# Q of batches 2 to 7 loaded four tokens to a partition, and read with a stride by the score matmuls

## The chip, the cores and the metric

One Trainium2 chip; the kernel runs on one of its cores. The metric is the time of one execution on the device, in microseconds. Before the change it was 320.49 us (median of 3 runs, 319.1 to 322.19). Runs of one kernel scatter by about 0.5%, so differences under 2% are read here only from several rounds on one chip.

## The reference

Sliding-window causal attention, then a two-layer MLP with a hard-swish gate. Cut to what matters:

```python
B, H, S, D = 8, 8, 576, 64            # q, k, v: [B, H, S, D] float32, about 0.1 in size
scores = (q @ k.T) / sqrt(D)          # only 0 <= query - key < 64 is kept
attn = softmax(scores) @ v            # per batch and head
x = attn.transpose(0, 2, 1, 3).reshape(B * S, H * D)     # 4608 tokens of 512
h = x @ w_in                          # w_in [512, 2048]
g = h * clip(h + 3, 0, 6) / 6
out = g @ w_out                       # w_out [2048, 512]
```

## The kernel before

Everything on TensorE is bf16. A batch has 576 tokens: 512 "main" ones (`SM`) and a tail of 64 (`SR`). The 4608 tokens pass through the MLP in nine blocks of 512. While block T is computed, the attention of batch T+1 is interleaved with it on TensorE, from T = 1 to 6; the last two blocks have no attention beside them.

Batches 0 and 1 are transposed by TensorE. Batches 2 to 7, the ones that the change touches, come in by DMA, are cast on GpSimd (`pcopy`) and transposed by DMA from `qn`, `kn` into `QT`, `KT`. These hold one row per head dimension (two heads on 128 partitions) and one column per token.

```python
P, R, SM, SR = 128, 4, 512, 64
QW = 192                               # queries that one block of 128 keys can see

def load_blocks(t, src, b, kbs, tail=0):
    ...                                # block kb: token kb*128 + p goes to partition p
        out.append(nc.sync.dma_start(
            out=t[p0 : p0 + ss, kb, :, :],
            in_=src[b, :, s0 : s0 + ss, :].rearrange("h s d -> s h d"),   # runs of 64 f32 = 256 B
        ))

def load_for_dma(b):                   # batches 2 to 7
    for n, src in (("qst", q), ("kst", k), ("vst", v)):
        t = stage.tile([P, KB, H, D], F32, name=n, tag=n)
        ins += load_blocks(t, src, b, range(KB), ...)

def transpose_by_dma(self):
    for n, T in ((qn_all, self.QT), (kn_all, self.KT)):
        nc.sync.dma_start_transpose(out=T[:]..., in_=n[:]...)

def scores(bt, g, u, ...):             # g: pair of heads; u: which half of the key blocks
    ...                                # (o0, k0, q0, n): column in PSUM, first key, first query, queries
    blocks = (
        ((0, 0, 0, QW), (QW, P, P, QW)),
        ((0, 2 * P, 2 * P, QW), (QW, 3 * P, 3 * P, P), (QW + P, S - P, SM, SR)),
    )[u]
    for o0, k0, q0, n in blocks:
        for h in range(2):             # heads on partitions 0-63 and 64-127: they run side by side
            nc.tensor.matmul(
                st[:, h, o0 : o0 + n],
                lhsT=bt.KT[h * D : (h + 1) * D, g, k0 : k0 + P],
                rhs=bt.QT[h * D : (h + 1) * D, g, q0 : q0 + n],     # contiguous columns
                ...)
    def exps():                        # ScalarE, PSUM -> SBUF
        nc.scalar.activation(out=pT[:, :, 2 * u : 2 * u + 2, 0:QW],
            in_=st[:, :, 0:w].rearrange("p h (k w) -> p h k w", k=2), func=EXP, scale=scale)
```

So a pair of heads needs ten score matmuls: five pairs with 192, 192, 192, 128 and 64 columns, 768 in all for each head. That the two of a pair run side by side shows in the trace: all ten take 0.44 us (below), and one after another, at the 0.42 ns per column of the MLP's matmuls (216 ns from start to start for 512), the 1536 columns would take 0.65.

The softmax here doesn't subtract the row's maximum and nothing guards it: scores larger than these inputs give would overflow.

Of the kernel before, what the change touches and what calls it, by code (L numbers as in the profile page):

```python
# [9 lines left out]
F32 = mybir.dt.float32  # L10
# [14 lines left out]
def kernel(  # L25
# [9 lines left out]
    nc = tc.nc  # L35
    P = nc.NUM_PARTITIONS
    B, H, S, D = q.shape
# [4 lines left out]
    KB = (S + P - 1) // P  # L42
    SP = KB * P
    R = 4
    SM = P * R
    SR = S - SM
# [4 lines left out]
    QW = P + WINDOW  # L51
# [4 lines left out]
    stage = ctx.enter_context(tc.tile_pool(name="stage", bufs=1))  # L56
# [31 lines left out]
    def load_blocks(t, src, b, kbs, tail=0):  # L88
        out = []
        for kb in kbs:  # L90
            s0 = kb * P
            ss = min(P, S - s0)
            p0 = tail if ss < P else 0
            out.append(nc.sync.dma_start(  # L94
                out=t[p0 : p0 + ss, kb, :, :],
                in_=src[b, :, s0 : s0 + ss, :].rearrange("h s d -> s h d"),
            ))
        return out

    def load_qk_for_pe(b, heads):  # L100
        qst = stage.tile([P, H, R * D], F32, name="qst", tag="qst")
        kst = stage.tile([P, H, R * D], F32, name="kst", tag="kst")
        rst = stage.tile([P, H, D], F32, name="rst", tag="rst")
        ins = []
        for h0 in range(0, H, heads):
            for dst, src in ((qst, q), (kst, k)):
                ins.append(nc.sync.dma_start(
                    out=dst[:, h0 : h0 + heads, :],
                    in_=src[b, h0 : h0 + heads, 0:SM, :].rearrange("h (p j) d -> p h (j d)", j=R),
                ))  # L110
            if h0 == 0:
                for i, src in enumerate((q, k)):
                    ins.append(nc.sync.dma_start(
                        out=rst[i * SR : (i + 1) * SR, :, :],
                        in_=src[b, :, SM:S, :].rearrange("h s d -> s h d"),
                    ))
        return (qst, kst, rst), ins
# [5 lines left out]

    def load_for_dma(b):
        sts, ins = [], []
        for n, src in (("qst", q), ("kst", k), ("vst", v)):
            t = stage.tile([P, KB, H, D], F32, name=n, tag=n)
            ins += load_blocks(t, src, b, range(KB), SR if src is v else 0)
            sts.append(t)
        return tuple(sts), ins  # L130

    ctx.enter_context(tc.manual_schedule())
    def load_first():
# [28 lines left out]
    def keep_busy(n):  # L162
# [11 lines left out]
        out=mask1[:], in_=mask1[:], pattern=[[1, QW]], compare_op=ISGE,  # L174
# [3 lines left out]
        out=mask1[:], in_=mask1[:], pattern=[[-1, QW]], compare_op=ISGE,  # L178
        fill=0.0, base=WINDOW - 1, channel_multiplier=1,
    )  # L180
    qn_all = consts.tile([P, NG, KB, 2, D], BF16, name="qn")
    kn_all = consts.tile([P, NG, KB, 2, D], BF16, name="kn")
# [3 lines left out]
    for o0, m0, m1 in ((0, 0, QW), (QW, 0, QW), (2 * QW, 0, QW), (3 * QW, 0, P), (3 * QW + P, WINDOW, P)):  # L186
        nc.vector.tensor_scalar(
            out=maskneg[:, o0 : o0 + m1 - m0], in0=mask1[:, m0:m1],
# [45 lines left out]
    vcopy, pcopy, acopy = nc.vector.tensor_copy, nc.gpsimd.tensor_copy, nc.scalar.copy  # L234

    class Batch:
# [10 lines left out]
            copy(out=self.V[SR:P, KB - 1, :, 0:D], in_=vst[SR:P, KB - 1, :, :])  # L247

        def cast_for_dma(self, st, which=(0, 1, 2)):
            for n, s in [((qn_all, st[0]), (kn_all, st[1]))[i] for i in which if i < 2]:  # L250
                for g in range(NG):
                    pcopy(  # L252
                        out=n[:, g, 0 : KB - 1, :, :].rearrange("p k h d -> p k (h d)"),
                        in_=s[:, 0 : KB - 1, 2 * g : 2 * g + 2, :].rearrange("p k h d -> p k (h d)"),
                    )
                pcopy(
                    out=n[:SR, :, KB - 1, :, :].rearrange("p g h d -> p g (h d)"),
                    in_=s[:SR, KB - 1, :, :].rearrange("p (g h) d -> p g (h d)", h=2),
                )
            if 2 in which:  # L260
                self.cast_v(st[2], 0, H, pcopy)
                self.cast_v_end(st[2], pcopy)
# [66 lines left out]
    def scores(bt, g, u, bias=False, bank=None):  # L329


        pT = P_ring[(bt.b * NG + g) % NPT]
        st = ps_st.tile([P, 2, 512], F32, name=f"st{u if bank is None else bank}")
        w = 2 * QW
        if bias:
            for h in range(2):
                nc.tensor.matmul(
                    st[:, h, 0:w], lhsT=ident[:], rhs=maskneg[:, u * w : (u + 1) * w],
                    start=True, stop=False,
                )  # L340
        blocks = (
            ((0, 0, 0, QW), (QW, P, P, QW)),
            ((0, 2 * P, 2 * P, QW), (QW, 3 * P, 3 * P, P), (QW + P, S - P, SM, SR)),
        )[u]
        for o0, k0, q0, n in blocks:
            for h in range(2):
                nc.tensor.matmul(  # L347
                    st[:, h, o0 : o0 + n],
                    lhsT=bt.KT[h * D : (h + 1) * D, g, k0 : k0 + P],
                    rhs=bt.QT[h * D : (h + 1) * D, g, q0 : q0 + n],  # L350
                    start=not bias, stop=not bias or o0 == blocks[-1][0],
                )

        def exps():
            nc.scalar.activation(  # L355
                out=pT[:, :, 2 * u : 2 * u + 2, 0:QW],
                in_=st[:, :, 0:w].rearrange("p h (k w) -> p h k w", k=2),
                func=EXP, scale=scale,
            )

        return exps
# [180 lines left out]
    def S_(bt, g, u):  # L542
        later[bt.b, "s", g, u] = scores(bt, g, u)
# [33 lines left out]
    bt, st = Batch(0), stage0  # L577
# [12 lines left out]
    def S0_(g, u):  # L590
        later[0, "s", g, u] = scores(bt, g, u, bias=True, bank=(u if g > 1 else g))
# [50 lines left out]
    st1, ins = load_qk_for_pe(1, 4)  # L642
    for x in ins:
# [5 lines left out]
        out=mask[:], in_=mask1[:].unsqueeze(1).to_broadcast([P, 2 * (KB - 1), QW])  # L649
    )  # L650
    for h in range(2):
        nc.vector.tensor_copy(
            out=mask[:, (KB - 1) * (h + 1) - 1, P:QW], in_=mask1[:, WINDOW : 2 * WINDOW],
        )
    bt, st = Batch(1), st1
# [14 lines left out]
    for g in range(NG):  # L670
        bt.cast_v(vst1, 2 * g, 2 * g + 2, pcopy)
    st2, _ = load_for_dma(2)

    m = s2(0, BY_QUARTER)
# [80 lines left out]
    for T in range(1, NTB):  # L755
        p1, p2 = pieces(nxt)
        b = T + 2
        nxt = None
        if b < B:
            sts, _ = load_for_dma(b)  # L760
            nxt = Batch(b)
            p1.setdefault(12 if T == 1 else 6, []).append(
                lambda bt=nxt, sts=sts: bt.cast_for_dma(sts)
            )
            p2.setdefault(6 if T == 1 else 12, []).append(lambda bt=nxt: bt.transpose_by_dma())
        stage_(T, None, p1, p2)
# [30 lines left out]
```

## Time and profile before

| | before |
|---|---|
| time, median | 320.49 us |
| span of the profiled run | 317.6 us |
| TensorE busy | 300.8 us (95%) |
| DMA packets under 512 B | 138272 |
| one full period (a block of the MLP and one batch of attention) | 32.0 us |
| ten score matmuls of a head pair | 0.44 us |

The first lines are from the profile's page: busy time of the engines, and the DMA packets.

```profile
PE 300.8 (95%) x2131; PEld 149.5 (47%) x2167; DVE 173.9 (55%) x331; ACT 177.9 (56%) x265; POOL 85.7 (27%) x131
...
DMA packets 150843, 52.64 MB, mean 166 GB/s; under 512 B 138272, under 2 KB 146464, under 8 KB 150816
```

The next are from the table of stretches of the same kernel: each line is a stretch (start and end in us), its length, then busy us and instructions of TensorE, its weight loads, VectorE, ScalarE and GpSimd, the granted clock of TensorE, the DMA share and GB/s. The first three stretches are full periods, the last is a block without attention.

```profile
162.53:194.57 32.04, 31.83 (x234) 15.85 (x237) 19.72 (x36) 19.17 (x29) 9.71 (x13) 1.00 1.04 203
194.57:226.60 32.03, 31.82 (x234) 15.87 (x237) 19.93 (x36) 19.17 (x29) 10.27 (x13) 1.00 1.02 201
226.60:258.64 32.04, 31.83 (x235) 15.86 (x237) 19.31 (x36) 19.17 (x29) 0.00 (x0) 1.00 0.37 79
258.64:286.27 27.63, 27.52 (x127) 12.54 (x128) 11.00 (x16) 13.34 (x20) 0.00 (x0) 1.00 0.10 39
```

TensorE has no gaps there. The first two stretches and the third take the same 32.0 us although the DMA share falls from 1.04 to 0.37: in this part DMA doesn't set the pace.

Where DMA does reach TensorE is the timeline of TensorE, in three places. Each line has start, length, what ran, and in brackets the idle time just before it and what ended that.

```profile
76.59 0.51 PE L347 MATMUL st<-QT,KT 64*128 64x192 bf16 x10 [0.43 <-DMA KT<-kn]
...
106.69 0.51 PE L347 MATMUL st<-QT,KT 64*128 64x192 bf16 x10 [1.97 <-DMA KT<-kn]
...
130.77 1.46 PE L466 MATMUL st<-xT,win 128*128 128x512 bf16 x6 [1.04 <-DMA xT<-opg]
```

These 3.4 us are what earlier loads could win. From 131 us on TensorE waits for no DMA. The price of a score group stands in the same timeline, inside a period:

```profile
171.96 0.51 PE L347 MATMUL st<-QT,KT 64*128 64x192 bf16 x10
172.40 1.04 PE L466 MATMUL hT<-xT,win 128*128 128x512 bf16 x3
```

A length (0.51) reaches past the next start (171.96 + 0.51 = 172.47), so lengths overlap; the cost is the distance of the two starts, 172.40 - 171.96 = 0.44 us for 768 columns.

### The profile page before, as it was taken

Reading aid. Unit: us, or ns where it says so; the run is one execution under the profiler, and the core shown is the slowest. Engines: PE = TensorE matmul, PEld = TensorE weight load, DVE = VectorE, ACT = ScalarE, POOL = GpSimd, SP = SyncE. Lnnn points to the kernel's source line nnn. Section 1 sums busy time; section 2 is a strip of 40 time slices with the busy share of each in tenths; the row PEclk is TensorE's granted clock in tenths of the full one; section 3 lists DMA queues with packets and bytes.
Section 4 is the critical chain, followed back from the end, with each engine's and each line's share of the span. In section 5 each row is a group of like instructions: output and inputs, shape, how many; then the busy total and the mean of one; then the engine's idle time right before and its main releaser. Section 6 shows DMA issues by size and latency. Waiting matters only on the chain.

```text
span 317.6 us, 5604 instructions
## 1 busy us (share of the span) xinstructions
PE 300.8 (95%) x2131; PEld 149.5 (47%) x2167; DVE 173.9 (55%) x331; ACT 177.9 (56%) x265; POOL 85.7 (27%) x131
## 2 busy tenths in 40 slices
PE   8989799999999799899999999999999999999995
PEld 3454345544554355344544554445444544444442
DVE  4658643476636665277527853785378438406700
ACT  2748753387637771487258725872587347417711
POOL 5741805363045143305610650065000000000000
PEclk9999999999999999999999999999999999999999
DMA  8999999999799999999999998999800630010011
GB/s 211 237 173 253 238 199 205 204 184 248 158 208 209 270 215 205 191 254 204 195 257 210 207 184 208 211 201 185 204 34 2 122 75 0 28 73 33 0 68 66
DMA packets 150843, 52.64 MB, mean 166 GB/s; under 512 B 138272, under 2 KB 146464, under 8 KB 150816
## 3 DMA queue, kind: packets, MB, share of 16 engines
q1 hardware_dynamic: 146000, 46.77, 72.7%
q0 software_dynamic: 4544, 5.24, 9.5%
q8 instruction: 17, 0.28, 0.4%
q10 hardware_dynamic: 272, 0.26, 0.2%
q14 instruction: 10, 0.08, 0.1%
HBM read 36.70 MB, written 9.44 MB: 145 GB/s over the span
## 4 chain that ended last, share of the span: by engine, by line
PE 63%; DMA 21%; SPq 8%; POOL 3%; issue 2%; DVE 1%; ACT 1%; POOLq 0%
PE o L503 15%; PE acc L503 14%; PE hT L466 14%; PE acc L466 5%; PE o L466 5%; SPq L94 5%; DMA vst<-in_v_dram 4%; DMA kst<-in_k_dram 4%; DMA KT<-kn 4%; DMA qst<-in_q_dram 3%; PE st L466 3%; PE st L347 3%; DMA wout<-in_moe_w_out_dram 3%; DMA win<-in_moe_w_in_dram 3%; PE hT L377 1%
## 5 line engine op out<-in xcount | busy, mean ns | idle before, releaser
L466 PEld LDWEIGHTS <-win 128*128 128x128 bf16 x576 | 55.3, 98 | 67.2 <-issue 2.3
L503 PEld LDWEIGHTS <-gT 128*128 128x128 bf16 x576 | 52.9, 98 | 57.5 <-issue 0.6
L503 PE MATMUL o<-wout,gT 128*128 128x512 bf16 x274 | 67.5, 379 | 1.5 <-DMA wout<-in_moe_w_out_dram 0.7
L503 PE MATMUL acc<-wout,gT 128*128 128x512 bf16 x278 | 67.1, 379 | 0.7 <-issue 0.3
L466 PE MATMUL hT<-xT,win 128*128 128x512 bf16 x266 | 65.7, 379 | 0.3
L355 ACT ACTIVATE pT<-st 128x768 bf16<-128x768 f32 x64 | 48.9, 813 | 10.8 <-PE st L347 10.7
L473 ACT ACTIVATE t<-hT,half 128x512 bf16<-128x512 f32 x68 | 46.7, 690 | 9.6 <-PE hT L466 9.2
L474 DVE SCALAR_TENSOR_TENSOR gT<-t,hT 128x512 bf16<-128x512 bf16 x68 | 46.4, 685 | 9.4 <-ACT t L473 9.1
L474 DVE SCALAR_TENSOR_TENSOR gT<-t,st 128x512 bf16<-128x512 bf16 (+1 forms) x26 | 19.7, 768 | 52.9 <-ACT t L473 52.9
L365 DVE TENSOR_TENSOR pT<-pT,mask 128x1536 bf16<-128x1536 bf16 x28 | 28.1, 1004 | 23.0 <-ACT pT L355 23.0
L509 ACT COPY osb<-o 128x512 f32<-128x512 f32 x18 | 10.6, 586 | 46.2 <-PE o L503 46.2
L252 POOL CAST qn<-qst 128x512 bf16<-128x512 f32 x24 | 16.1, 712 | 74.1 <-DMA qst<-in_q_dram 59.7
L509 ACT COPY osb<-acc 128x512 f32<-128x512 f32 x18 | 10.6, 587 | 35.7 <-PE acc L503 33.7
L466 PE MATMUL st<-xT,win 128*128 128x512 bf16 x117 | 28.2, 379 | 1.7 <-DMA xT<-opg 1.0
L397 DVE TENSOR_TENSOR opg<-hT,rec 128x320 bf16<-128x320 f32 x56 | 27.5, 492 | 1.9
L466 PE MATMUL acc<-xT,win 128*128 128x512 bf16 x91 | 23.6, 379 | 0.1
L466 PE MATMUL o<-xT,win 128*128 128x512 bf16 x90 | 23.5, 379 | 0.1
L473 ACT ACTIVATE t<-st,half 128x512 bf16<-128x512 f32 (+1 forms) x26 | 19.4, 752 | 7.2 <-PE st L466 7.1
L377 PEld LDWEIGHTS <-pT 128*128 128x128 bf16 x256 | 17.8, 97 | 9.1 <-issue 1.4
L347 PE MATMUL st<-QT,KT 64*128 64x192 bf16 (+2 forms) x320 | 17.9, 229 | 4.2 <-DMA KT<-kn 2.4
L394 DVE RECIPROCAL rec<-hT 128x5 f32<-128x5 f32 x56 | 10.5, 188 | 20.0 <-PE hT L386 19.9
L243 POOL CAST V<-vst 128x512 bf16<-128x512 f32 (+1 forms) x14 | 16.4, 1168 | 17.4 <-DMA vst<-in_v_dram 17.0
(76 smaller groups left out, 269.2 us busy)
## 6 DMA issues: line engine op xcount, KB each, us to landing
out_dram<-osb SPq DMA_DIRECT2D x32, 256.0 KB, 2.4
qst<-in_q_dram SPq DMA_DIRECT2D x28, 256.0 KB, 4.7
kst<-in_k_dram SPq DMA_DIRECT2D x27, 256.0 KB, 5.4
vst<-in_v_dram SPq DMA_DIRECT2D x24, 256.0 KB, 5.1
vst<-in_v_dram SPq DMA_DIRECT2D x24, 128.0 KB, 4.1
win<-in_moe_w_in_dram POOLq DMA_DIRECT2D x4, 512.0 KB, 7.6
wout<-in_moe_w_out_dram POOLq DMA_DIRECT2D x4, 512.0 KB, 8.8
qst<-in_q_dram SPq DMA_DIRECT2D x2, 512.0 KB, 6.1
```

Source lines behind the costliest of these rows:

```text
L243: copy(out=self.V[:, 0 : KB - 1, h0:h1, 0:D], in_=vst[:, 0 : KB - 1, h0:h1, :])
L252: pcopy(out=n[:, g, 0 : KB - 1, :, :].rearrange("p k h d -> p k (h d)"), in_=s[:, 0 : KB - 1, 2 * g : 2 * g + 2, :].rearrange("p k h d -> ...
L347: nc.tensor.matmul(st[:, h, o0 : o0 + n], lhsT=bt.KT[h * D : (h + 1) * D, g, k0 : k0 + P], rhs=bt.QT[h * D : (h + 1) * D, g, q0 : q0 + n], ...
L355: nc.scalar.activation(out=pT[:, :, 2 * u : 2 * u + 2, 0:QW], in_=st[:, :, 0:w].rearrange("p h (k w) -> p h k w", k=2), func=EXP, scale=scale,
L365: nc.vector.tensor_tensor(out=pT[:, :, :, 0:QW], in0=pT[:, :, :, 0:QW], in1=mask[:].rearrange("p (h k) w -> p h k w", h=2), op=MULT,)
L377: nc.tensor.matmul(ob, lhsT=pT[:, h, qb, 0:P], rhs=V[:, qb, 2 * g + h, :], start=True, stop=(qb == 0),)
L397: nc.vector.tensor_tensor(out=opgs[bt.b, g][:, :, h, :], in0=ov[:, :, 0:D], in1=rec[:].unsqueeze(2).to_broadcast([P, KB, D]), op=MULT,)
L466: nc.tensor.matmul(hT, lhsT=win16[:, g, fc * P : (fc + 1) * P], rhs=xT[:, g, t0 : t0 + TB], start=(g == 0), stop=(g == NG - 1),)
L473: nc.scalar.activation(out=t1[:], in_=hT, func=RELU, bias=half[:], scale=1.0 / 6.0)
L474: nc.vector.scalar_tensor_tensor(out=out, in0=t1[:], scalar=1.0, in1=hT, op0=MIN, op1=MULT,)
L503: nc.tensor.matmul(accs[ts], lhsT=gT[:, fc, ts * P : (ts + 1) * P], rhs=wout16[:, fc, :], start=(fc == 0), stop=(fc == NFC - 1),)
L509: nc.scalar.copy(out=osb[:], in_=accs[ts])
```

## The change

The intent is fewer, longer packets. If partition p takes the four consecutive tokens 4p to 4p+3, each head gives one run of 1 KB in place of four of 256 B, and three loads of Q are issued in place of five. The price is the order: after the DMA transpose token 4s+j stands in column 128j+s. The scores undo this by reading Q^T with a step of 128 columns (256 bytes) for j within s. The 64 tail tokens stay in natural order. K and V stay as they were.

```diff
     def load_for_dma(b):
-        for n, src in (("qst", q), ("kst", k), ("vst", v)):
+        qst = stage.tile([P, H, R * D], F32, name="qst", tag="qst")
+        rst = stage.tile([P, H, D], F32, name="rst", tag="rst")
+        for h0 in range(0, H, 4):
+            ins.append(nc.sync.dma_start(
+                out=qst[:, h0 : h0 + 4, :],
+                in_=q[b, h0 : h0 + 4, 0:SM, :].rearrange("h (p j) d -> p h (j d)", j=R),
+            ))
+        ...  # the tail into rst
+        for n, src in (("kst", k), ("vst", v)):
...
             # cast_for_dma
+                        pcopy(
+                            out=n[:, g, 0 : KB - 1, :, :],
+                            in_=st[0][0][:, 2 * g : 2 * g + 2, :].rearrange("p h (j d) -> p j h d", j=R),
+                        )
...
             # scores
+        if bt.b > 1:
+            for i in range(2):
+                for h in range(2):
+                    kb = 2 * u + i
+                    n = min(QW, SM - kb * P)
+                    nc.tensor.matmul(
+                        st[:, h, i * QW : i * QW + n].rearrange("p (s j) -> p s j", j=R),
+                        lhsT=bt.KT[h * D : (h + 1) * D, g, kb * P : (kb + 1) * P],
+                        rhs=bt.QT[h * D : (h + 1) * D, g, 0:SM].rearrange(
+                            "d (j s) -> d s j", j=R
+                        )[:, kb * P // R : (kb * P + n) // R, :],
+                        start=True, stop=True,
+                    )
+            ...  # the 64-column tail, contiguous, as before
-        for o0, k0, q0, n in blocks:
+        for o0, k0, q0, n in blocks if bt.b < 2 else ():
```

The matmuls and weight loads are the same ones in the same order; only the access pattern of one operand differs.

More of the change, by code (lines that the diff above doesn't have):

```diff
@@ L125, in load_for_dma @@
         sts, ins = [], []
-        for n, src in (("qst", q), ("kst", k), ("vst", v)):
+        qst = stage.tile([P, H, R * D], F32, name="qst", tag="qst")
[5 more added lines that the diff above has]
+            ))
+        ins.append(nc.sync.dma_start(
+            out=rst[0:SR, :, :], in_=q[b, :, SM:S, :].rearrange("h s d -> s h d"),
+        ))
+        for n, src in (("kst", k), ("vst", v)):
             t = stage.tile([P, KB, H, D], F32, name=n, tag=n)
@@ L129, in load_for_dma @@
             sts.append(t)
-        return tuple(sts), ins
+        return ((qst, rst), *sts), ins
     ctx.enter_context(tc.manual_schedule())
@@ L249, in cast_for_dma @@
         def cast_for_dma(self, st, which=(0, 1, 2)):
-            for n, s in [((qn_all, st[0]), (kn_all, st[1]))[i] for i in which if i < 2]:
+            for i in which:
+                if i > 1:
+                    continue
+                n = (qn_all, kn_all)[i]
                 for g in range(NG):
-                    pcopy(
-                        out=n[:, g, 0 : KB - 1, :, :].rearrange("p k h d -> p k (h d)"),
-                        in_=s[:, 0 : KB - 1, 2 * g : 2 * g + 2, :].rearrange("p k h d -> p k (h d)"),
-                    )
+                    if i:
+                        pcopy(
+                            out=n[:, g, 0 : KB - 1, :, :].rearrange("p k h d -> p k (h d)"),
+                            in_=st[1][:, 0 : KB - 1, 2 * g : 2 * g + 2, :].rearrange("p k h d -> p k (h d)"),
+                        )
+                    else:
+                        pcopy(
+                            out=n[:, g, 0 : KB - 1, :, :],
+                            in_=st[0][0][:, 2 * g : 2 * g + 2, :].rearrange("p h (j d) -> p j h d", j=R),
+                        )
+                rest = st[1][:SR, KB - 1, :, :] if i else st[0][1][:SR, :, :]
                 pcopy(
                     out=n[:SR, :, KB - 1, :, :].rearrange("p g h d -> p g (h d)"),
-                    in_=s[:SR, KB - 1, :, :].rearrange("p (g h) d -> p g (h d)", h=2),
+                    in_=rest.rearrange("p (g h) d -> p g (h d)", h=2),
                 )
@@ L340, in scores @@
                 )
+        if bt.b > 1:
[10 more added lines that the diff above has]
+                        start=True, stop=True,
+                    )
+            if u:
+                for h in range(2):
+                    nc.tensor.matmul(
+                        st[:, h, QW + P : 2 * QW],
+                        lhsT=bt.KT[h * D : (h + 1) * D, g, S - P : S],
+                        rhs=bt.QT[h * D : (h + 1) * D, g, SM:S],
+                        start=True, stop=True,
+                    )
         blocks = (
```

## The prediction

> **What bounds the kernel now.** TensorE: 300.8 of 317.6 us busy (95%, busy table). In the table of stretches each full period from 162 us on (one token block of the MoE plus one batch of attention) lasts 32.0 us with PE busy 31.8, at full clock. PE's 17 us of idle time lie before 131 us. DMA looks full there (share about 1 until 230 us), but only three of PE's waits are ones that Q loading can touch (timeline of PE): 0.43 us before the first scores of batch 2 (76.6 us, released by the K transpose), 1.97 us before those of batch 3 (106.7 us, same releaser), 1.04 us at 130.8 us (released by the transpose into xT). Together 3.4 us.
>
> **What it removes.** For each of six batches, the 1 MB main part of Q goes from 4096 packets of 256 B to 1024 of 1 KB. In the trace's packets of the hardware queue these take 22.5 and 57 ns on average, so 5.8 us of the sixteen engines become 3.6 (an estimate). SyncE issues three Q loads in place of five (5 to 6 us a batch in its timeline; I expect 2.5 to 4). K, V and the transposes behind them should come 2 to 3 us sooner, enough to erase the three waits: about -3 us. After 131 us an earlier load is worth nothing.
>
> **What it moves.** Nothing in order: the same matmuls and weight loads; GpSimd's reordered Q cast has the form that takes 0.62 us in batch 0.
>
> **What it adds.** The moving operand of the scores of batches 2 to 7 is read in steps of 256 bytes, apart from the 64-column tail. The ten score matmuls of a head pair take 0.44 us (timeline): five pairs side by side, 768 columns, 704 of them now strided; 24 groups x 704 = 16,900 columns, 7.0 us at 2.4 columns per ns. Four of the six batches lie wholly in the PE-bound part and pay in full. The Trainium skill, "SBUF — State Buffer", note on cachelines, says that each access to a new 16-byte line pays a penalty and that two hits per line are needed to absorb the latency; it gives no figure for TensorE. No instruction of this trace reads a strided moving operand, so this is the gamble:
> - no penalty: about 317.5 us (chance 0.3)
> - half rate: +0.29 us per group, +7.0 - 3.2, about 324 (0.4)
> - quarter rate or worse: +21 - 3, about 338 (0.25)
> - between: 0.05
>
> **Prediction.** 323.5 us, 8 in 10 between 316.5 and 336. Faster by over 2%: 0.03; within 2%: 0.70; slower by over 2%: 0.27.
>
> **What would show each step.** Packets under 512 B fall by about 24,600, under 2 KB by 18,400. The waits at 76, 106 and 130 us shrink below 0.3 us each. Score groups of batches 2 to 7: 0.44 us if the stride is free, about 0.73 at half rate, 1.3 at quarter rate; the period 32.0, 33.2 or 35.5 us. The last two blocks, without attention, stay at 27.6 us each.
>
> **What would make it wrong.** The stride costing more than half rate, or breaking the side-by-side running of two heads; the two-level step pattern costing extra; 1 KB pieces draining no faster because HBM binds; a much slower cast on GpSimd.

## The result, and the profile after

338.19 us (median of 4 runs, 336.26 to 339.52) against 321.34 us before (median of 4, 319.1 to 322.19); ratio 1.0531, 95% interval 1.0448 to 1.0615. A ratio here is the mean time of one kernel's fast runs over the mean of the other's of the same rounds, so it is not quite the ratio of the medians. The change is slower by 5%, outside the predicted range (316.5 to 336).

The page of the kernel after, the same two lines:

```profile
PE 321.9 (96%) x2131; PEld 152.1 (45%) x2167; DVE 174.9 (52%) x331; ACT 182.1 (54%) x265; POOL 87.1 (26%) x131
...
DMA packets 132219, 52.64 MB, mean 157 GB/s; under 512 B 113504, under 2 KB 127840, under 8 KB 132192
```

The packets fell as meant, by 24,768 under 512 B. TensorE is busy 21.1 us longer with the same 2131 recorded matmuls. The table of stretches of the kernel after, three full periods and the block without attention:

```profile
169.34:204.90 35.56, 35.35 (x235) 16.28 (x237) 20.09 (x36) 20.02 (x29) 10.34 (x13) 1.00 0.79 181
204.90:240.45 35.55, 35.34 (x234) 16.26 (x237) 19.62 (x36) 20.02 (x29) 10.33 (x13) 1.00 0.85 181
240.45:276.00 35.55, 35.34 (x235) 16.25 (x237) 19.57 (x36) 20.02 (x29) 0.00 (x0) 1.00 0.31 72
276.00:303.63 27.63, 27.52 (x128) 12.54 (x128) 11.00 (x16) 13.33 (x20) 0.00 (x0) 1.00 0.10 39
```

A period with attention takes 3.5 us more; the block without attention takes exactly what it took. The timeline of TensorE after, one score group (the tail now has a line of its own):

```profile
178.77 1.35 PE L366 MATMUL st<-QT,KT 64*128 64x192 bf16 x8
179.95 0.21 PE L376 MATMUL st<-QT,KT 64*128 64x64 bf16 x2
180.09 1.04 PE L507 MATMUL hT<-xT,win 128*128 128x512 bf16 x3
```

The group takes 180.09 - 178.77 = 1.32 us in place of 0.44. Its 704 strided columns take 1.18 us, 1.68 ns each; 24 groups x 0.88 us = 21.1 us. The spans differ by 335.3 - 317.6 = 17.7 us, 3.4 us less, which is what the three waits were; all three are gone (the same three places, now without a bracket):

```profile
76.46 1.35 PE L366 MATMUL st<-QT,KT 64*128 64x192 bf16 x8
...
107.67 1.35 PE L366 MATMUL st<-QT,KT 64*128 64x192 bf16 x8
...
133.63 1.89 PE L507 MATMUL st<-xT,win 128*128 128x512 bf16 x8
```

That the sum closes to a tenth is partly luck: other waits moved as well (for V from GpSimd 2.1 us in place of 1.3), and in this execution the granted clock was 0.93 and 0.90 from 30 to 40 and from 40 to 50 us, where it had been 1.00. It looks as if the loads had paid their part. The experiments show that this reading is only half right.

### The profile page after: what moved, and what is told of

The parts are those of the page before. It is cut to its first block, busy times and chain, and to the rows that moved or that the text cites. A ratio compares the mean times of both kernels' runs of the same rounds, so it can differ in the third digit from the quotient of the medians.

```text
span 335.3 us, 5584 instructions
## 1 busy us (share of the span) xinstructions
PE 321.9 (96%) x2131; PEld 152.1 (45%) x2167; DVE 174.9 (52%) x331; ACT 182.1 (54%) x265; POOL 87.1 (26%) x131
## 4 chain that ended last, share of the span: by engine, by line
PE 85%; DMA 7%; ACT 2%; SPq 2%; issue 1%; DVE 1%; POOL 1%; POOLq 0%
PE o L544 19%; PE acc L544 18%; PE hT L507 16%; PE st L366 9%; PE acc L507 6%; PE o L507 6%; PE st L507 5%; DMA win<-in_moe_w_in_dram 2%; DMA kst<-in_k_dram 2%; PE hT L418 2%; PE hT L423 1%; DMA vst<-in_v_dram 1%; DMA qst<-in_q_dram 1%; PE hT L448 1%; DVE gT L515 1%
## 5 line engine op out<-in xcount | busy, mean ns | idle before, releaser
L544 PE MATMUL o<-wout,gT 128*128 128x512 bf16 x274 | 68.3, 382 | 1.0 <-issue 0.2
L271 POOL CAST qn<-qst 128x512 bf16<-128x512 f32 x24 | 14.8, 645 | 72.8 <-DMA qst<-in_q_dram 72.8
L366 PE MATMUL st<-QT,KT 64*128 64x192 bf16 x192 | 32.5, 469 | 0.0
L266 POOL CAST kn<-kst 128x512 bf16<-128x512 f32 x24 | 16.6, 729 | 28.1 <-DMA kst<-in_k_dram 24.0
```

The source lines that it names most:

```text
L266: pcopy(out=n[:, g, 0 : KB - 1, :, :].rearrange("p k h d -> p k (h d)"), in_=st[1][:, 0 : KB - 1, 2 * g : 2 * g + 2, :].rearrange("p k h d ...
L271: pcopy(out=n[:, g, 0 : KB - 1, :, :], in_=st[0][0][:, 2 * g : 2 * g + 2, :].rearrange("p h (j d) -> p j h d", j=R),)
L366: nc.tensor.matmul(st[:, h, i * QW : i * QW + n].rearrange("p (s j) -> p s j", j=R), lhsT=bt.KT[h * D : (h + 1) * D, g, kb * P : (kb + 1) ...
L544: nc.tensor.matmul(accs[ts], lhsT=gT[:, fc, ts * P : (ts + 1) * P], rhs=wout16[:, fc, :], start=(fc == 0), stop=(fc == NFC - 1),)
```

## The experiments

In all of them "strided" means the read of Q^T in steps of 128 columns. The comparison with the reference passed for every run, also for those that take the tokens in a wrong order: q and k are so small that the softmax weights are nearly equal and the order hardly shows in the output. So a pass says little about the order here. The kernel before and three of these were therefore also evaluated in a simulation of their values (not of their times), with q and k 15 times larger: the relative error was 0.0055 for the kernel before and for both kernels below that are meant to be right (`e_act`, `e_psumw`), and 1.09 for `e_contig`, which is meant to be wrong. When this document was checked, the simulation was repeated: it gave the same figures, and 0.0055 for the change itself.

The theory: the stepped read costs TensorE time by itself. Rivals: the new loads or casts cost it; any two-level pattern costs it; the two heads no longer run side by side.

### The loads alone: `e_contig`

```diff
-    st[:, h, i * QW : i * QW + n].rearrange("p (s j) -> p s j", j=R),
+    st[:, h, i * QW : i * QW + n],
     lhsT=bt.KT[h * D : (h + 1) * D, g, kb * P : (kb + 1) * P],
-    rhs=bt.QT[..., g, 0:SM].rearrange("d (j s) -> d s j", j=R)[:, kb * P // R : (kb * P + n) // R, :],
+    rhs=bt.QT[h * D : (h + 1) * D, g, kb * P : kb * P + n],      # wrong order on purpose
```

> The change's loads (1 KB runs of Q), but the scores of batches 2 to 7 read Q^T without a stride, so the tokens stand in the wrong order and the result is wrong on purpose. Theory (the strided read costs, the loads help a little): score groups back at 0.44 us, period 32.0 us, the waits at 76, 106 and 130 us gone or under 0.5 us, time about 318 us, ratio to before 0.985 to 0.995. Rival (the new loads, casts or their contention cost the time): about 338 us, ratio 1.05, with score groups at 0.44 us and waits elsewhere. Rival 2 (the waits vanished only because the slower scores delay TensorE): ratio 0.997 to 1.003, the waits still there.

Measured: 317.55 us (6 runs) against 320.44 us; ratio 0.9905, interval 0.9861 to 0.9948. TensorE waits for no K transpose and no transpose into xT in the whole run. The scores of batch 3 start here with no wait before them:

```profile
104.21 1.03 PE L505 MATMUL hT<-xT,win 128*128 128x512 bf16 x4
105.17 0.48 PE L366 MATMUL st<-QT,KT 64*128 64x192 bf16 x8
105.48 0.19 PE L374 MATMUL st<-QT,KT 64*128 64x64 bf16 x2
```

The K transpose of batch 2 was issued at 69.06 us and landed 6.6 us later, before 76.16 us, when TensorE had been ready for it in the kernel before (76.59 less the wait of 0.43).

What follows: the new loads cost nothing and win about 1% when the scores are not slowed. The rivals "the loads cost" and "the waits vanish only because TensorE is late" both fall for this kernel.

### The stride alone: `e_stride_only`

```diff
 # the kernel before, with its own loads and casts
+        if bt.b > 1:
+            ...  # the strided score matmuls of the change; wrong order on purpose
-        for o0, k0, q0, n in blocks:
+        for o0, k0, q0, n in blocks if bt.b < 2 else ():
```

> The loads of before, with the strided read of the scores in batches 2 to 7 (wrong token order, wrong result on purpose). Theory: score groups 1.3 us, period 35.5 us, time about 338 to 341 us, ratio 1.053 to 1.065, at or a little above the whole change, because the waits at 76 and 130 us may stay. Rival (the loads cost): about 321 us, ratio 1.00.

Measured: 338.83 us (4 runs) against 320.44 us; ratio 1.0561, interval 1.0505 to 1.0617. This is the whole loss. More: it is the time of the whole change (1.0531, interval 1.0448 to 1.0615), with the loads of before, and here too no wait for a K transpose or for xT is left on TensorE. The scores of batch 3 start at 109.47 us in place of 106.69, right behind the matmuls ahead of them; slower scores of batch 2 have made TensorE late enough for the old loads (the first line is the first scores of batch 2):

```profile
78.26 1.36 PE L346 MATMUL st<-QT,KT 64*128 64x192 bf16 x8
...
108.51 1.03 PE L487 MATMUL hT<-xT,win 128*128 128x512 bf16 x4
109.47 0.81 PE L346 MATMUL st<-QT,KT 64*128 64x192 bf16 x4
```

What follows: the two effects are not a sum. The stride alone removes the two longer waits, 1.97 and 1.04 us. The third, 0.43 us before the first scores of batch 2, comes ahead of every strided read, so its absence here is not the stride's doing: in this execution TensorE was 2.2 us late already at the last scores of batch 1 (49.30 us against 47.07; the granted clock was 0.83 from 40 to 50 us, against 1.00). The better loads remove all three, but once the stride has removed two, the 0.4 us that is left is less than these runs could show. The two ratios come from different jobs, so a difference of some tenths of a per cent stays open.

### Which patterns cost: `e_sweep`

Each of the 24 score groups reads Q^T with another pattern, in one run; matmul counts and sizes are unchanged.

```diff
+    STEPS = {  # by batch and head pair
+        (2, 0): ("step", 1), (2, 1): ("step", 2), (2, 2): ("step", 3), (2, 3): ("far", 128, 4),
+        (3, 0): ("step", 1), (3, 1): ("step", 4), (3, 2): ("step", 6), (3, 3): ("step", 8),
+        (4, 0): ("step", 5), (4, 1): ("step", 7), (4, 2): ("step", 12), (4, 3): ("step", 13),
+        (5, 0): ("runs", 4, 8), (5, 1): ("runs", 2, 8), (5, 2): ("runs", 2, 12), (5, 3): ("runs", 4, 32),
+        (6, 0): ("far", 4, 48), (6, 1): ("far", 8, 24), (6, 2): ("far", 32, 6), (6, 3): ("far", 64, 4),
+        (7, 0): ("h0",), (7, 1): ("h1",), (7, 2): ("long",), (7, 3): ("keys",),
+    }
-                        rhs=bt.QT[...].rearrange("d (j s) -> d s j", j=R)[...],
+                        rhs=rhs,       # built from STEPS; wrong order on purpose
```

"step n" is one column in n; "runs m, n" is m contiguous columns in every n; "far n, m" has steps of n columns inside and of one column outside; "long" is four runs of 48 (or 32) columns, 128 apart; "h0" and "h1" stride one head only (by 128); "keys" reads the stationary K in steps of 13 columns and Q without.

> The change's loads, and in each of the 24 score groups of batches 2 to 7 another access pattern of the moving operand (wrong result on purpose). A group's eight 192- and 128-column matmuls (704 columns in pairs) take about 0.33 us from the first start to the start of the tail at full rate, 0.6 at half and 1.18 at quarter rate. Theory A (every access that opens a new 16-byte line costs four column times): steps of 2, 3 and 4 elements 0.33 us, or up to 0.6 for 4; steps of 8, 12 and 13 all 1.18; two-level patterns with 2 or 4 elements per line 0.33 to 0.6; four runs of 48 with 128 between them 0.33; four elements 8 or more apart 1.18. Theory B (the two-level step pattern costs, whatever the distance): single steps of 8 to 13 0.33, all two-level ones 1.18. Theory C (the two heads no longer run side by side and each goes at half rate): groups in which only one head is strided about 0.16 x 3.7 + 0.08 x 3.7 = 0.9 us; under A they take 1.18, the slower head's time. A strided stationary operand (last group) with contiguous moving: 0.33 to 0.5.

Measured, as the distance from the first start of the eight wide matmuls (704 columns) to the start of the tail:

| pattern | bf16 columns per 16-byte line | us | ns per column |
|---|---|---|---|
| step 1; long | 8 | 0.31 to 0.32 | 0.45 |
| runs 4, 8 and 4, 32 | 4 | 0.32 | 0.45 |
| step 3 | 2.7 | 0.48 | 0.68 |
| step 4; runs 2, 8 and 2, 12; far 4 | 2 | 0.61 to 0.62 | 0.87 |
| step 5 | 1.6 | 0.76 | 1.08 |
| step 6 | 1.3 | 0.92 | 1.31 |
| step 7 | 1.1 | 1.08 | 1.53 |
| step 8, 12, 13; far 8 | 1 | 1.22 to 1.26 | 1.73 to 1.79 |
| far 32, 64, 128 | 1 | 1.17 to 1.18 | 1.66 to 1.68 |
| keys (stationary strided) | 8 (moving) | 0.35 | 0.50 |

Step 2 (4 columns per line) had a wait on ScalarE in the middle, so it gives only a part: its last 320 columns took 0.14 us, 0.44 ns each. Theory A had put a step of 3 at 0.33 us; it took 0.48. Whole lines for step 4 and step 8 of this run:

```profile
112.02 0.79 PE L410 MATMUL st<-QT,KT 64*128 64x192 bf16 x8
112.63 0.21 PE L420 MATMUL st<-QT,KT 64*128 64x64 bf16 x2
...
118.86 1.41 PE L410 MATMUL st<-QT,KT 64*128 64x192 bf16 x8
120.09 0.21 PE L420 MATMUL st<-QT,KT 64*128 64x64 bf16 x2
```

What follows: the cost is that of a line, not of a stride. A line of 16 bytes costs about 1.7 ns, the time of four columns at full rate (216 ns start to start for 512 columns is 0.42 ns each), and its columns are free up to four. Steps that give one column per line cost about four times the full rate's time (1.66 to 1.79 ns against 0.45), whether the step is 16 bytes or 256. That a pattern has two levels costs nothing ("runs 4, 8", "long"). With one head strided the wide matmuls and the tails of the group took 246.11 - 244.79 = 1.32 us, as with both, and so did the group with the other head strided. If the heads excluded each other, then of the wide matmuls' time with both strided each head would have half, at half the rate, and a head read at the full rate would need only half of its half: three quarters in all. In that group one head's tail even starts before the other head's last wide matmuls:

```profile
244.79 0.81 PE L410 MATMUL st<-QT,KT 64*128 64x192 bf16 x6
245.11 0.20 PE L420 MATMUL st<-QT,KT 64*128 64x64 bf16 x1
245.43 0.72 PE L410 MATMUL st<-QT,KT 64*128 64x192 bf16 x2
245.97 0.20 PE L420 MATMUL st<-QT,KT 64*128 64x64 bf16 x1
246.11 1.04 PE L551 MATMUL hT<-xT,win 128*128 128x512 bf16 x3
```

The Trainium skill, "SBUF — State Buffer", note on cachelines, asks for two hits per line. For TensorE's moving operand in bf16 two hits gave half the rate and 2.7 two thirds of it; four gave the full rate. The strided stationary operand ("keys") is not free either. Its eight weight loads took 136 ns in the median against 94 in the group "long" (from the view of the tile KT; shortest/median/longest in ns, first and last start in us, "keys" first); of that, 0.04 us reached the group, which took 0.35 us against 0.31:

```profile
L410 PEld LDWEIGHTS <-KT x8: 136/136/157, 256.4 to 256.7; 64*128 64x128 bf16 x8
...
L410 PEld LDWEIGHTS <-KT x8: 92/94/95, 252.8 to 253.0; 64*128 64x128 bf16 x8
```

The time of this run (330.51 us, one look) is that of a mixture and isn't used.

### The stride moved to the write into PSUM: `e_psumw`

```diff
-    st[:, h, i * QW : i * QW + n].rearrange("p (s j) -> p s j", j=R),
+    st[:, h, i * QW : i * QW + n].rearrange("p (s j) -> p j s", j=R),
-    rhs=bt.QT[...].rearrange("d (j s) -> d s j", j=R)[:, kb * P // R : (kb * P + n) // R, :],
+    rhs=bt.QT[...].rearrange("d (j s) -> d j s", j=R)[:, :, kb * P // R : (kb * P + n) // R],
```

> The change's loads with a correct result: TensorE reads Q^T as four runs of 48 (or 32) tokens and writes the scores to PSUM with a step of four columns (16 bytes), so PSUM holds the natural order and the exponential stays as it was. If only the reading of SBUF by lines costs: about 318 us, ratio 0.987 to 0.997, score groups 0.44 us. If a stepped write to PSUM costs TensorE too, as the Trainium skill (Advanced Engine Details and Errata, PSUM Cachelines) says of any non-contiguous pattern: half rate 0.75 us per group and about 325 us; quarter rate 1.3 us and about 338 us.

Measured: 325.07 us (4 runs) against 319.75 us; ratio 1.0169, interval 1.0122 to 1.0215. A group in the timeline of TensorE:

```profile
179.11 0.77 PE L366 MATMUL st<-QT,KT 64*128 64x192 bf16 x8
179.68 0.23 PE L376 MATMUL st<-QT,KT 64*128 64x64 bf16 x2
179.85 1.04 PE L507 MATMUL hT<-xT,win 128*128 128x512 bf16 x4
```

704 columns take 0.57 us, 0.81 ns each. So writing PSUM in steps of four float32 columns nearly halves TensorE's rate (the read in runs of 48 cost nothing in the sweep, pattern "long"). The skill's "Advanced Engine Details and Errata", section PSUM Cachelines, says that any non-contiguous pattern slows matmuls significantly; here the size is a factor of 1.8. It is cheaper than the strided read and still a loss.

### The stride moved to ScalarE: `e_act`, and `e_act_again`

TensorE reads runs of 48 and writes them as they come; the exponential, which has to read PSUM anyway, picks the natural order. The tail is read in steps of 4 columns so that one exponential still serves the half group (that part of the edit is cut, as is the old exponential kept for batches 0 and 1).

```diff
-    st[:, h, i * QW : i * QW + n].rearrange("p (s j) -> p s j", j=R),
+    st[:, h, 2 * i * P : 2 * i * P + QW].rearrange("p (j s) -> p j s", j=R)[:, :, 0 : n // R],
-    rhs=bt.QT[...].rearrange("d (j s) -> d s j", j=R)[:, kb * P // R : (kb * P + n) // R, :],
+    rhs=bt.QT[...].rearrange("d (j s) -> d j s", j=R)[:, :, kb * P // R : (kb * P + n) // R],
...
     nc.scalar.activation(
         out=pT[:, :, 2 * u : 2 * u + 2, 0:QW],
-        in_=st[:, :, 0:w].rearrange("p h (k w) -> p h k w", k=2),
+        in_=st[:].rearrange("p h (k w) -> p (h k) w", k=2)[:, :, 0:QW].rearrange("p x (j s) -> p x s j", j=R),
```

> The change's loads with a correct result and no single-element stride for TensorE: the moving operand is read as four runs of 48 (or 32) tokens, the scores stand in PSUM in that order, and the exponential on ScalarE reads PSUM with a stride and writes the natural order. Only the 64-column tail is read in steps of 4 elements (8 bytes). Theory: score groups 0.44 to 0.5 us, the exponential within 10% of its 0.81 us, time about 318 us, ratio 0.985 to 0.997, equal to the run with the wrong order. If ScalarE pays for a strided read of PSUM (say 1.6 us in place of 0.81), the time is 320 to 326 and waits on the exponential appear on TensorE. If any two-level pattern costs TensorE: about 338.

Measured: five runs of 316.94 to 318.69 us, and one, the profiled one, of 1097.17 us. Over the fast runs the ratio is 0.9921, interval 0.9878 to 0.9964. In the odd execution every matmul was slow, those of the MLP too: a 512-column one followed another after about 0.80 us (four from 304.84 to 308.04 us) in place of 0.216. ScalarE was not slow: its exponential took 808 ns (before 813). Its profile can't be compared, so the kernel ran again.

> The same kernel as the run in which ScalarE undoes the order, again, because the profile of that run fell on one execution of 1097 us, with matmuls of 1091 ns in place of 379 ns on TensorE, while its other five took 317 to 319 us. If that execution was an accident of the chip, all executions now take 317 to 319 us, ratio 0.987 to 0.997, score groups 0.44 to 0.5 us, the exponential 0.81 us (up to 0.9), no wait of TensorE on a K transpose. If the kernel itself provokes it, it should come again in about one of six.

Measured: six runs of 316.15 to 319.12 us, median 316.9, against 319.75; ratio 0.9915, interval 0.9879 to 0.9952; no odd execution among the six. One in twelve is not enough to say what caused it, and that stays open. "TensorE: Matmul & The Clock Gate" (HAM trace caveats) reports a clock gate seen stuck at a quarter; by an estimate from that page's 2.4 GHz a quarter would give 512 columns in 0.85 us, near the 0.80 seen. But the page of that execution, alone of the eight, has no line of the granted clock (PEclk), its trace holds no record of it, and the 1.00 that other views print there is no measurement. So the trace neither shows this nor rules it out.

A group and the exponentials in the second profile (timeline of TensorE, then the line of the groups by form: busy us, mean ns, idle before):

```profile
168.70 0.48 PE L366 MATMUL st<-QT,KT 64*128 64x192 bf16 x8
169.02 0.22 PE L376 MATMUL st<-QT,KT 64*128 64x64 bf16 x2
169.16 1.04 PE L514 MATMUL hT<-xT,win 128*128 128x512 bf16 x4
```

```profile
L403 ACT ACTIVATE pT<-st 128x768 bf16<-128x768 f32 x48 | 36.1, 810 | 1.6 <-PE st L366 1.6
```

The group takes 0.46 us. The exponential takes 810 ns; before it took 813. ScalarE reads PSUM in steps of 192 bytes for nothing. So this version has the loads of the change and is the fastest with the right order that was tried: 0.8% under the kernel before, in two jobs on two chips, equal within the intervals to `e_contig`. That is less than the 2% that would call it faster.

## Why the prediction was wrong, point by point

- **What bounds the kernel**: right. TensorE; the block without attention kept its 27.6 us, and the DMA share in a period fell from about 1.03 to about 0.82 without any gain.
- **Packets**: right, 24,768 fewer under 512 B against about 24,600 foreseen, and 18,624 fewer under 2 KB against 18,400.
- **The gain of the loads, about 3 us**: right in size when alone (`e_contig`, 320.44 to 317.55 us). Beside the cost of the stride the subtraction came out right by luck: I took off 3.2 us for the loads, and `e_stride_only` shows that the stride alone removes the two longer waits, 3.0 us of the 3.4, with the old loads. Nothing that the loads do shows in the time of the whole change.
- **The cost of the stride**: this is the step that failed, the term of the sum that was mis-sized. As the prediction put it: "half rate: +0.29 us per group, +7.0 - 3.2, about 324 (0.4)". Measured, a group takes 0.88 us more, 21.1 us over 24 groups: a quarter of the rate, the branch that I had given 0.25. The mechanism, a new 16-byte line at every access, was the right one; I took "two hits per line" to mean that one hit halves the rate. No run had shown it, and the sweep says that the full rate of the moving operand needs four bf16 columns per line, so that one gives a quarter.
- **The two heads side by side, the two-level pattern, the cast on GpSimd** as sources of error: none of them. With one head strided the group takes the strided head's time; "long" and "runs 4, 8" cost nothing; the Q casts took 645 ns on average against 712 before, far from the critical path.

The range failed for a plainer reason as well: a quarter of the weight lay on a branch at 338 us that had been written down, and the upper end of 336 left it out.

## What to carry to other kernels

Put a necessary reordering on an engine and a memory for which it is free: here ScalarE's read of PSUM, not TensorE's read of SBUF (four times) or its write to PSUM (1.8 times). In a matmul count the 16-byte lines of the moving operand and not its columns; four bf16 columns per line are enough. And before adding a gain to a cost, ask whether both act on the same waits, because a slower engine hides late data as well as an earlier load does.

## What the Trainium skill lacked or had wrong

- "SBUF — State Buffer", note on cachelines (and "Advanced Engine Details and Errata", SBUF Cachelines): it asks for at least two hits per line and gives no rate for TensorE. With a bf16 moving operand two columns per 16-byte line gave half the rate (0.87 ns per column), one gave a quarter (1.66 to 1.79), four the full (0.45).
- The same note says that one can step up to 8 bf16 for free. Steps of 3 and 4 elements already cost 0.68 and 0.87 ns per column, and a step of 8 costs 1.75.
- "Advanced Engine Details and Errata", PSUM Cachelines: "significantly slows down matmuls" has no size. A write in steps of 16 bytes took 0.81 ns per column against 0.45. Neither that section nor "ScalarE: Activation LUTs" has what was seen on ScalarE: a read of PSUM in steps of 192 bytes took 810 ns against 813 contiguous.
- "TensorE: Matmul & The Clock Gate" says of fast weight load that columns may be packed or strided, and gives no price for the stride. In one group a stationary operand in steps of 26 bytes lengthened the weight loads from 94 ns to 136 (medians) and the group from 0.31 us to 0.35; whether these loads are of the fast kind the trace doesn't say.
- No page has an execution in which every matmul ran at about a quarter of its speed (0.80 us for 512 columns in place of 0.216) for the whole 1095 us, with no record of the granted clock in its trace; the longest that "TensorE: Matmul & The Clock Gate" tells of is 50 us and more.
